# Attention with a tanh cap and a spectral mix: sums of exponentials in halves in two early slots, and a later tanh in one slot of each batch

## The chip, the cores and the metric

The kernel runs on one core of one Trainium2 chip. The metric is the device time of one execution in microseconds (us). A time quoted for a kernel is the median of several runs, and a profile is one execution of its own. A difference of about 0.2% (1.9 us here) is what a measurement of this kernel can tell from none.

## The reference

There are 8 batches of 12 heads, 448 positions and a head size of 64, all in float32. The core of the computation is:

```python
scores = cap * np.tanh(scale * (q @ k.T) / cap)
attn = np.exp(scores - scores.max(-1)); attn /= attn.sum(-1) + 1e-9
x = attn @ v                       # heads side by side: 448 x 768 per batch
theta = x @ w_theta
y = w_tok_r @ (x * cos(theta)) + w_tok_i @ (x * sin(theta))
u = x + y
out = u + np.maximum(u @ w_ch, 0)
```

For a cap of at most 64 the kernel leaves the subtraction of the maximum out (the cap is 30 here). The products of the second half use each float32 operand as a rounded part and a remainder, so one product takes three matmuls.

## The kernel before

**Slots.** The program is one written order of work, cut into slots. Slot s computes the scores of head pair s, in two halves of two key chunks each. The name s2_1 means the second half of pair 2. Slot s also multiplies the exponentials of pair k = s - 1 with the values (`av`, tile `a`) and adds up their sums (`sums`, tile `r`) by matmuls with a matrix of ones. There are 48 head pairs, six to a batch. Slots 0 to 7 are the opening (`start`): no batch is complete yet, and the vector engine splits the weights for the later products into rounded part and remainder (tags th, ch and tk in the table `WEIGHTS`). From slot 8 on, six slots make up one batch of the second half, with `part` 0 to 5. Part 2 (slots 10, 16, 22, ... 46) holds the second group of transposes and the first mixing products.

**Order.** The schedule is manual: each engine (PE for matmuls, ACT for activations, DVE for vector work, SP for issuing transfers) runs its instructions in the order in which the code records them, and waits where an operand or a buffer isn't ready. So an instruction that is recorded late holds nothing ahead of it, and one that waits holds everything behind it on its engine.

**Buffers.** The score tile `s` has one buffer of four PSUM banks. The matmuls of the next half can start only when the tanh (L219) has read the half before. The other PSUM tiles (`a`, `r`, `th`, `t`, `mx`, `ch`) share four single banks in turn. The tiles `p` of exponentials have two tags of three buffers: `p`, and `xhl`, which is also used for the split x. The function `apart` says which pairs of the first batch take `xhl`. The tiles `bc` have two buffers.

**The sums of the first batch.** For the first six pairs, two pairs share one tile `r`. In slots 2, 4 and 6 (k odd) the sums of both pairs are made: a group of 16 matmuls from the first halves ahead of the second scores, and a group from the second halves behind them. The reciprocal `ri` (L296, `invert`) follows in the same slot on DVE, four transfers spread it over the partitions (`bc`, L300), and `norm` (L304) multiplies x by it. After that `split_x` (L313 on ACT, L314 on DVE) makes the rounded x and its remainder: pairs 0 to 3 at the end of slot 6, pairs 4 and 5 at the end of slot 7.

**Part 2.** After the second scores come seven transposes of z (`t`, L355), the rounding of their result by ACT (`zh`, L356), the remainder by DVE (`zl`, L357), the reciprocal, and the mixing products (`mx`, L364 to L366), 21 matmuls each. On ACT the tanh of the second scores stands ahead of the rounding.

Of the kernel before, what the change touches and what calls it, by code (L numbers as in the profile page):

```python
# [16 lines left out]
AF = mybir.ActivationFunctionType  # L17
# [15 lines left out]
WHOLE = 14  # L33
# [3 lines left out]
def softcap_attn_then_spectral_mix(ctx, tc, qk2, v, cap, w_theta, w_tok, w_ch, ident, outT):  # L37
    nc = tc.nc
    B, NP, P, _, S = qk2.shape
    D = P // 2  # L40
    CP = v.shape[2]
# [4 lines left out]
    NS = B * NP  # L46
# [14 lines left out]
    qscale = const.tile([P, 1], F32, name="qscale")  # L61
# [20 lines left out]
    def fill(n):  # L82

        t = psM.tile([P, 512], F32, tag="m", name=f"fill{len(fills)}")
        fills.append(t)
        for _ in range(n):
            nc.tensor.matmul(t[:32, :CP], ones_sb, ones_sb[:, :1].broadcast_to([CP, CP]), start=True, stop=True)
# [8 lines left out]
    class Split:  # L96
# [20 lines left out]
        def split(self):  # L117
            t, hi, lo, hw, lw = self.t, self.hi, self.lo, self.hw, self.lw
            ti = t.bitcast(I32)
            nc.vector.tensor_scalar(ti, hw.bitcast(I32), 3, None, op0=ALU.logical_shift_left)  # L120
            nc.vector.scalar_tensor_tensor(ti, hw.bitcast(I32), -(2**31), ti, op0=ALU.bitwise_and, op1=ALU.bitwise_or)
            nc.vector.tensor_scalar(hw.bitcast(I32), ti, -(2**23), None, op0=ALU.bitwise_and)
            nc.vector.scalar_tensor_tensor(lw, lw.bitcast(U32), 2.0**-52, hw, op0=ALU.mult, op1=ALU.mult)
            if self.act:
                nc.scalar.copy(hi, t)
            else:
                nc.vector.tensor_copy(hi, t)
            nc.vector.tensor_tensor(t, t, hi.bitcast(F32), op=ALU.subtract)
            nc.vector.tensor_tensor(lo, t, lw, op=ALU.add)
# [35 lines left out]
    def weights(s, pos):  # L165
        for word in WEIGHTS.get((s, pos), "").split():
            step = steps[word[-3:-1], int(word[-1])]
            {">": step.load, "*": step.scale, "#": step.vscale}.get(word[0], step.split)()
# [4 lines left out]
    state = {}  # L173
# [3 lines left out]
    def load_qk(k):  # L177

        if 0 < k < WHOLE:
            raw[k] = wk.tile([P, 2, S], F32, tag=("hi", "lo")[k % 2], name=f"qk{k}", bufs=1)  # L180
        else:
            raw[k] = qk_sb
        nc.sync.dma_start(raw[k], qk2[k // NP, k % NP])

    def load_v(k):
        vt[k] = wk.tile([CP, 2, NCH, D], F32, tag="v", name=f"v{k}", bufs=2)
        nc.sync.dma_start(vt[k], v[k // NP, k % NP])
# [7 lines left out]
        if k + 1 < NS:  # L195
            load_qk(k + 1)

    def apart(k):


        return k < NP and k % 2 == 0

    def qk_half(k, half):

        sp = psS.tile([P, 2, 2, 512], F32, tag="s", name=f"s{k}_{half}")
        if apart(k):
            pp = wk.tile([CP, 2, 2, S], F32, tag="xhl", name=f"p{k}_{half}", bufs=3)
        else:
            pp = wk.tile([CP, 2, 2, S], F32, tag="p", name=f"p{k}_{half}", bufs=3)
        pt[k, half] = pp  # L210
        for i in range(2):
            ks = slice((2 * half + i) * CP, (2 * half + i + 1) * CP)
            products = ((raw, raw),) if k < WHOLE else ((hi, hi), (lo, hi), (hi, lo))
            for n, (kk, qq) in enumerate(products):
                for hh in range(2):
                    rows = slice(hh * D, (hh + 1) * D)
                    nc.tensor.matmul(sp[:CP, i, hh, :S], kk[k][rows, 1, ks], qq[k][rows, 0, :],  # L217
                                     start=n == 0, stop=n == len(products) - 1)
        nc.scalar.activation(pp, sp[:CP, :, :, :S], AF.Tanh, scale=qscale[:CP])  # L219

    def exp_half(k, half):

# [40 lines left out]
    def sum_pairs(ks, r, halves=(0, 1)):  # L263

        if ks[0] in pst:
            addends = [([pst.pop(k) for k in ks], True, True)]
        else:
            addends = [([pt[k, c // 2][:, c % 2] for k in ks], c == 0, c == NCH - 1) for c in range(NCH) if c // 2 in halves]
        for tiles, start, stop in addends:
            for k, a in zip(ks, tiles):  # L270
                for hh in range(2):
                    i = 2 * (k % 2) + hh
                    nc.tensor.matmul(r[32 * i : 32 * i + 32, :S], ones_sb, a[:, hh, :], start=start, stop=stop)  # L273

    def sums(k, halves=(0, 1)):

        alone = state["general"] or NP <= k < DIRECT
        if not alone and k % 2 == 0:
            return
        if state["general"] and 0 not in halves:  # L280
            return
        if (k % 2 == 0 or not alone) and 0 in halves:
            state["r"] = psM.tile([P, 512], F32, tag="m", name=f"r{k}")
        sum_pairs((k,) if alone else (k - 1, k), state["r"], halves)

    def invert(k):

        if k % 2 == 0:
            return
        r = state.pop("r")  # L290
        ri = wk.tile([P, S], F32, tag="ri", name=f"ri{k}", bufs=1)
        if state["general"]:
            nc.vector.tensor_scalar_add(ri, r[:, :S], 1e-9)
            nc.vector.reciprocal(ri, ri)
        else:
            nc.vector.reciprocal(ri, r[:, :S])  # L296
        for n in (k - 1, k):
            bc[n] = wk.tile([P, S], F32, tag="bc", name=f"bc{n}", bufs=2)
            for i in range(2):
                nc.sync.dma_start(bc[n][i::2, :], ri[D * (n % 2) : D * (n % 2) + D, :])  # L300
# [92 lines left out]
    def us(b, j):  # L393
        split_x(b, j, "us")

    def pipeline(general):
        state["general"] = general
        load_v(0)
        load_qk(1)
        for step in (("tk", 0), ("tk", 1)):  # L400
            steps[step].load()

        for s in range(FIRST + 6 * B):
            k = s - 1
            b, part = divmod(s - FIRST, 6)
            live = s < NS
            start = s < FIRST
            if s == 0:
                fill(FILL["first scores"])
            if live:  # L410
                qk_half(s, 0)
            if s == 0:
                fill(FILL["half"])
            if start:
                weights(s, "a")
                exp_half(s, 0)
            if 0 <= k < NS:
                av(k)
            if not start:
                weights(s, "a")  # L420
            if not start and part == 4:
                for j in range(NJ // 2, NJ):
                    us(b, j)
            if s + 1 < NS:
                load_v(s + 1)
            if 0 <= k < NS:
                sums(k, (0,) if start else (0, 1))
                if not start and part != 2:
                    invert(k)
            if live:  # L430
                qk_half(s, 1)
            if s == 0:
                fill(FILL["slot"])
            if 0 <= k and start:
                sums(k, (1,))
            if s + 2 <= WHOLE:
                load_qk(s + 2)
            if WHOLE <= s + 1 < NS and (start or part != 2):
                prep(s + 1)
            weights(s, "b")  # L440
            if 0 <= k and start:
                invert(k)
            script = ["B", "a", "b"] if start else part_scripts(b)[part]
            for i, e in enumerate(script):
                if not start and i == len(script) - 1:
                    weights(s, "c")
                    if s % 2 == 1 and s <= NS + 1:
                        norm(s - 3)
                        norm(s - 2)
                if isinstance(e, str):  # L450
                    if live:
                        if e in "AB":
                            exp_half(s, "AB".index(e))
                        else:
                            add_half(s, "ab".index(e))
                else:
                    e[0](b, e[1])
                if part == 2 and i == 0 and not start:
                    if 0 <= k < NS:
                        invert(k)  # L460
                    if WHOLE <= s + 1 < NS:
                        prep(s + 1)
            if start:
                weights(s, "c")
                for n in {4: (0, 1), 5: (2, 3), 7: (4, 5)}.get(s, ()):
                    norm(n)
                for j in {6: range(4), 7: range(4, NJ)}.get(s, ()):
                    split_x(0, j, "xs")
# [53 lines left out]
```

## Time and profile before

| what | value |
|---|---|
| median of 3 runs | 964.53 us (964.43 to 966.29) |
| the profiled execution's own time | 966.27 us |
| its span, first to last instruction | 964.5 us |
| PE busy | 945.6 us (98%) |
| DVE busy | 640.8 us (66%) |
| ACT busy | 590.5 us (61%) |
| granted TensorE clock | 0.997 |
| transfers | 68.68 MB, mean 71 GB/s |

The busy share of PE is near its limit over the whole span, so what remains to be looked at are the few places where PE sits idle. A row of the timeline has the start, the length, the engine, the line, the operation and its tiles, and in brackets how long the engine sat idle before it and what ended that. The ends of matmuls are modelled, so lengths of PE rows overlap, and distances between the starts of rows are the safer measure.

### The profile page before, as it was taken

The numbers are of one execution on the slowest core, as the hardware profiler recorded it, in microseconds if no ns is written. First come the engines' busy times: TensorE is split into PE (matmuls) and PEld (weight loads), VectorE is DVE, ScalarE is ACT, GpSimd is POOL, SyncE is SP. The second block draws the span as 40 slices with busy tenths as digits, with TensorE's granted clock in tenths as the row PEclk, the third lists the DMA queues.
The fourth block names the chain that finished last, engine by engine and source line by source line (L and its number), as shares of the span: only waits on it lengthen the run. The fifth ranks groups of instructions, "written<-read, shape, count | busy, mean of one in ns | idle before, by whom it ended". The sixth has DMA issues, their size and how long they took to land.

```text
span 964.5 us, 12776 instructions
## 1 busy us (share of the span) xinstructions
PE 945.6 (98%) x5224; PEld 697.3 (72%) x5224; DVE 640.8 (66%) x877; ACT 590.5 (61%) x609; POOL 0.4 (0%) x6
## 2 busy tenths in 40 slices
PE   8999999999999999999999999999999999999997
PEld 4234766677778777777787687767777877789897
DVE  5998787885855757756766559656585576664541
ACT  6888784667654687546963578456775558722520
POOL 0000000000000000000000000000000000000000
PEclk9999999999999999999999999999999999999999
DMA  7564122330113212132122221033011321001001
GB/s 252 193 194 138 34 82 94 112 103 30 49 39 105 67 39 63 32 98 67 32 66 68 77 67 48 29 87 94 31 49 39 105 68 39 20 15 62 0 1 61
DMA packets 30739, 68.68 MB, mean 71 GB/s; under 512 B 4304, under 2 KB 16720, under 8 KB 30672
## 3 DMA queue, kind: packets, MB, share of 16 engines
q1 hardware_dynamic: 30672, 67.78, 23.0%
q8 instruction: 43, 0.70, 0.3%
q14 instruction: 24, 0.20, 0.1%
HBM read 45.74 MB, written 11.01 MB: 59 GB/s over the span
## 4 chain that ended last, share of the span: by engine, by line
PE 88%; DVE 6%; ACT 4%; issue 1%; POOL 0%; POOLq 0%
PE a L257 15%; PE s L217 14%; PE mx L364 6%; PE mx L366 6%; PE mx L365 6%; PE th L322 6%; PE ch L322 6%; PE ch L324 6%; PE th L323 6%; PE ch L323 6%; PE th L324 6%; PE t L355 3%; PE r L273 3%; ACT p L219 2%; DVE ri L296 2%
## 5 line engine op out<-in xcount | busy, mean ns | idle before, releaser
L219 ACT ACTIVATE p<-s,qscale 112x1792 f32<-112x1792 f32 x96 | 168.7, 1757 | 168.7 <-PE s L217 168.7
L225 ACT ACTIVATE p<-p,cap_sb 112x1792 f32<-112x1792 f32 x96 | 170.6, 1790 | 0.6
L257 PE MATMUL a<-p,v 112*64 112x448 f32 x768 | 154.9, 545 | 0.0
L364 PE MATMUL mx<-wtk_h,zh 128*128 128x448 f32 x336 | 126.8, 377 | 5.4 <-DVE ri L296 3.6
L366 PE MATMUL mx<-wtk_h,zl 128*128 128x448 f32 x336 | 123.6, 368 | 0.0
L365 PE MATMUL mx<-wtk_l,zh 128*128 128x448 f32 x336 | 123.5, 367 | 0.0
L257 PEld LDWEIGHTS a<-p,v 112*64 112x64 f32 x768 | 50.9, 136 | 86.9 <-issue 77.1
L322 PE MATMUL th<-xs,wth_h 128*128 128x448 f32 x288 | 106.9, 371 | 0.0
L322 PE MATMUL ch<-us,wch_h 128*128 128x448 f32 x288 | 106.8, 371 | 0.0
L324 PE MATMUL ch<-us,wch_l 128*128 128x448 f32 x288 | 105.5, 366 | 0.0
L323 PE MATMUL th<-xs,wth_h 128*128 128x448 f32 x288 | 105.4, 366 | 0.0
L323 PE MATMUL ch<-us,wch_h 128*128 128x448 f32 x288 | 105.3, 366 | 0.0
L324 PE MATMUL th<-xs,wth_l 128*128 128x448 f32 x288 | 105.3, 366 | 0.0
L250 DVE TENSOR_TENSOR ps<-ps,p 112x896 f32<-112x896 f32 x80 | 87.0, 1087 | 1.4
L296 DVE RECIPROCAL ri<-r 128x448 f32<-128x448 f32 x24 | 70.8, 2952 | 12.0 <-PE r L273 11.9
L335 DVE SCALAR_TENSOR_TENSOR g_sb<-g_sb 128x448 f32<-128x448 f32 x48 | 29.9, 624 | 65.8 <-ACT g_sb L334 65.4
L364 PEld LDWEIGHTS mx<-wtk_h,zh 128*128 128x128 f32 x336 | 63.6, 189 | 11.9 <-issue 5.0
L357 DVE TENSOR_TENSOR zl<-t,zh 128x512 fp32r<-128x512 f32 x96 | 55.2, 616 | 24.5 <-ACT zh L356 24.5
L375 DVE SCALAR_TENSOR_TENSOR x<-ch,x 128x448 f32<-128x448 f32 x48 | 29.8, 620 | 59.0 <-PE ch L324 59.0
L366 PEld LDWEIGHTS mx<-wtk_h,zl 128*128 128x128 f32 x336 | 63.5, 189 | 5.4
L365 PEld LDWEIGHTS mx<-wtk_l,zh 128*128 128x128 f32 x336 | 63.7, 190 | 4.9
L322 PEld LDWEIGHTS ch<-us,wch_h 128*128 128x128 f32 x288 | 54.1, 188 | 9.6 <-issue 4.6
(75 smaller groups left out, 1377.8 us busy)
## 6 DMA issues: line engine op xcount, KB each, us to landing
qk_sb<-in_qk SPq DMA_DIRECT2D x35, 448.0 KB, 3.4
v<-in_v SPq DMA_DIRECT2D x48, 224.0 KB, 2.5
bc<-ri SPq DMA_DIRECT2D x96, 112.0 KB, 2.3
out_dram<-x SPq DMA_DIRECT2D x48, 224.0 KB, 1.9
qk<-in_qk SPq DMA_DIRECT2D x13, 448.0 KB, 3.4
g_sb<-in_wth SPq DMA_DIRECT2D x6, 768.0 KB, 5.4
g_sb<-in_wch SPq DMA_DIRECT2D x6, 768.0 KB, 4.7
swk_raw<-in_wtok SPq DMA_DIRECT2D x7, 448.0 KB, 4.1
```

Of the source, the lines that this page charges most:

```text
L217: nc.tensor.matmul(sp[:CP, i, hh, :S], kk[k][rows, 1, ks], qq[k][rows, 0, :], start=n == 0, stop=n == len(products) - 1)
L219: nc.scalar.activation(pp, sp[:CP, :, :, :S], AF.Tanh, scale=qscale[:CP])
L225: nc.scalar.activation(pp, pp, AF.Exp, scale=cap_sb[:CP])
L250: nc.vector.tensor_tensor(pst[k], pst[k], pt[k, 1][:, i], op=ALU.add)
L257: nc.tensor.matmul(acc[hh * D : (hh + 1) * D, :S], va[:, hh, c, :], pt[k, c // 2][:, c % 2, hh, :], start=c == 0, stop=c == NCH - 1)
L296: nc.vector.reciprocal(ri, r[:, :S])
L322: nc.tensor.matmul(acc[:, :S], wh[:, j, ms], t[:, 0, :], start=j == 0, stop=False)
L323: nc.tensor.matmul(acc[:, :S], wh[:, j, ms], t[:, 1, :], start=False, stop=False)
L324: nc.tensor.matmul(acc[:, :S], wl[:, j, ms], t[:, 0, :], start=False, stop=j == NJ - 1)
L364: nc.tensor.matmul(acc[:, :S], zh[:, c, :], wtk_h[:, c, :], start=c == 0, stop=False)
L365: nc.tensor.matmul(acc[:, :S], zh[:, c, :], wtk_l[:, c, :], start=False, stop=False)
L366: nc.tensor.matmul(acc[:, :S], zl[:, c, :], wtk_h[:, c, :], start=False, stop=c == NC2 - 1)
```

## The change

It has two parts.

**Sums in halves.** For pairs 0 and 1, and for pairs 2 and 3 (`split`: k = 1 and k = 3), the group from the first halves now stands behind the second scores of slots 2 and 4, and the group from the second halves behind the second scores of the slots after, 3 and 5. The reciprocal moves one slot later with them. The products `norm` of pairs 2 and 3 move from slot 5 to slot 6. The tiles of exponentials live longer for it, and `apart` gives other halves the tag `xhl`.

**Tanh later.** In part 2 the tanh of the second scores is recorded after the first group of transposes, behind the rounding of their result. This holds in the seven slots 10, 16, ... 46, which have scores of their own.

```diff
-    def apart(k):
-        return k < NP and k % 2 == 0
+    def apart(k, half):
+        return (k, half) in ((0, 0), (0, 1), (2, 0), (3, 0), (4, 0), (5, 0), (5, 1))
...
-        nc.scalar.activation(pp, sp[:CP, :, :, :S], AF.Tanh, scale=qscale[:CP])
+        return lambda: nc.scalar.activation(pp, sp[:CP, :, :, :S], AF.Tanh, scale=qscale[:CP])
...
+    def split(k):
+        return k in (1, 3) and not state["general"]
...
-                sums(k, (0,) if start else (0, 1))
+                if not start or not split(k):
+                    sums(k, (0,) if start else (0, 1))
                 if not start and part != 2:
                     invert(k)
+            late = not start and part == 2
             if live:
-                qk_half(s, 1)
+                tanh = qk_half(s, 1)
+                if not late:
+                    tanh()
...
             if 0 <= k and start:
-                sums(k, (1,))
+                if split(k):
+                    sums(k, (0,))
+                elif split(k - 1):
+                    sums(k - 1, (1,))
+                else:
+                    sums(k, (1,))
...
-            if 0 <= k and start:
-                invert(k)
+            if 0 <= k and start and not split(k):
+                invert(k - 1 if split(k - 1) else k)
...
-                if part == 2 and i == 0 and not start:
+                if late and i == 0:
+                    if live:
+                        tanh()
                     if 0 <= k < NS:
                         invert(k)
...
-                for n in {4: (0, 1), 5: (2, 3), 7: (4, 5)}.get(s, ()):
+                for n in {4: (0, 1), 6: (2, 3), 7: (4, 5)}.get(s, ()):
                     norm(n)
```

On PE, slots 2 and 3 before (each row of `r` stands twice, once for each head of a pair; the repeats are left out):

```order
L273 MATMUL r1_254<-p0_0_133,ones_sb_83 32x448 x2
L273 MATMUL r1_254<-p1_0_184,ones_sb_83 32x448 x2
...
L217 MATMUL s2_1_263<-qk2_170 112x448 x4
L273 MATMUL r1_254<-p0_1_153,ones_sb_83 32x448 x2
L273 MATMUL r1_254<-p1_1_205,ones_sb_83 32x448 x2
...
L217 MATMUL s3_0_298<-qk3_211 112x448 x4
L257 MATMUL a2_307<-p2_0_233,v2_202 64x448 x4
L257 MATMUL a2_307<-p2_1_264,v2_202 64x448 x4
L217 MATMUL s3_1_320<-qk3_211 112x448 x4
L217 MATMUL s4_0_349<-qk4_278 112x448 x4
```

and now:

```order
L217 MATMUL s2_1_254<-qk2_170 112x448 x4
L273 MATMUL r1_261<-p0_0_133,ones_sb_83 32x448 x2
L273 MATMUL r1_261<-p1_0_184,ones_sb_83 32x448 x2
...
L217 MATMUL s3_0_282<-qk3_211 112x448 x4
L257 MATMUL a2_291<-p2_0_233,v2_202 64x448 x4
L257 MATMUL a2_291<-p2_1_255,v2_202 64x448 x4
L217 MATMUL s3_1_304<-qk3_211 112x448 x4
L273 MATMUL r1_261<-p0_1_153,ones_sb_83 32x448 x2
L273 MATMUL r1_261<-p1_1_205,ones_sb_83 32x448 x2
...
L217 MATMUL s4_0_349<-qk4_270 112x448 x4
```

Slot 2 has one group of sums in place of two, and slot 3 one in place of none. Slots 4 and 5 read the same way.

On DVE, around the end of slot 6 before, from the last step of a weight split (L129) to the remainders of x:

```order
L129 TENSOR_TENSOR wth_l_78<-g_sb1_87 128x6x128
L296 RECIPROCAL ri5_526<-r5_492 128x448
L314 TENSOR_TENSOR xs0_0_536<-x0_200,xs0_0_536 128x448
L314 TENSOR_TENSOR xs0_0_536<-x1_250,xs0_0_536 128x448
L314 TENSOR_TENSOR xs0_2_541<-x2_316,xs0_2_541 128x448
```

and now, where the lines of the changed kernel are L300 for the reciprocal, L308 for `norm` and L318 for the remainders:

```order
L129 TENSOR_TENSOR wth_l_78<-g_sb1_87 128x6x128
L300 RECIPROCAL ri5_524<-r5_490 128x448
L308 TENSOR_TENSOR x2_300<-bc2_461,x2_300 128x448
L308 TENSOR_TENSOR x3_367<-bc3_464,x3_367 128x448
L318 TENSOR_TENSOR xs0_0_536<-x0_200,xs0_0_536 128x448
L318 TENSOR_TENSOR xs0_0_536<-x1_250,xs0_0_536 128x448
```

The products of pairs 2 and 3 now stand behind the third reciprocal, and ACT's rounding of x2 and x3 (not shown, its order is unchanged) needs them. The second reciprocal, ri3, now stands where these products stood, ahead of the last split of w_theta.

On ACT, slot 16 (part 2) before:

```order
L260 COPY x15_1780<-a15_1771 128x448
L219 ACTIVATE p16_1_1790<-s16_1_1789,qscale_70 112x1792
L356 CAST zh1_1_1804<-t1_1_0_1806 128x512
L356 CAST zh1_1_1804<-t1_1_4_1813 128x384
L341 ACT_TABLE_LOAD
```

and now:

```order
L260 COPY x15_1780<-a15_1771 128x448
L360 CAST zh1_1_1803<-t1_1_0_1805 128x512
L360 CAST zh1_1_1803<-t1_1_4_1812 128x384
L219 ACTIVATE p16_1_1790<-s16_1_1789,qscale_70 112x1792
L345 ACT_TABLE_LOAD
```

One instruction has moved past two, and nothing else on ACT has moved in the whole program. PE and DVE keep their order in these slots.

More of the change, by code (lines that the diff above doesn't have):

```diff
@@ L196, in prep @@
             load_qk(k + 1)
-    def apart(k):
-        return k < NP and k % 2 == 0
+    def apart(k, half):
+        return (k, half) in ((0, 0), (0, 1), (2, 0), (3, 0), (4, 0), (5, 0), (5, 1))
     def qk_half(k, half):
         sp = psS.tile([P, 2, 2, 512], F32, tag="s", name=f"s{k}_{half}")
-        if apart(k):
+        if apart(k, half):
             pp = wk.tile([CP, 2, 2, S], F32, tag="xhl", name=f"p{k}_{half}", bufs=3)
@@ L410, in pipeline @@
             if live:
-                qk_half(s, 0)
+                qk_half(s, 0)()
             if s == 0:
@@ L434, in pipeline @@
             if 0 <= k and start:
-                sums(k, (1,))
+                if split(k):
[4 more added lines that the diff above has]
+                    sums(k, (1,))
             if s + 2 <= WHOLE:
                 load_qk(s + 2)
-            if WHOLE <= s + 1 < NS and (start or part != 2):
+            if WHOLE <= s + 1 < NS and (not late):
                 prep(s + 1)
             weights(s, "b")
-            if 0 <= k and start:
-                invert(k)
+            if 0 <= k and start and not split(k):
+                invert(k - 1 if split(k - 1) else k)
             script = ["B", "a", "b"] if start else part_scripts(b)[part]
```

## The prediction

> **What bounds the kernel now.** I read the page first, then the list of waits of PE, then the timeline at the places that the list names.
>
> ```profile
> PE 945.6 (98%) x5224; PEld 697.3 (72%) x5224; DVE 640.8 (66%) x877; ACT 590.5 (61%) x609; POOL 0.4 (0%) x6
> PE s L217 <- ACT p L219: 6.7, 7, 1.9
> PE mx L364 <- DVE ri L296: 3.6, 7, 0.5
> ```
>
> PE is busy for 98% of the span, so only its idle time can be won. The two wait rows (total us, times, longest) hold most of that idle time. Both belong to places that the change touches: the next scores waiting for a tanh, and a mixing product waiting for a reciprocal.
>
> **Sums in halves, the PE side.** These are the rows of slots 2 to 5 on PE and ACT.
>
> ```profile
> 27.95 1.71 PE L273 MATMUL r<-p,ones_sb 112*32 112x448 f32 x16
> 29.59 1.76 PE L217 MATMUL s<-qk 64*112 64x448 f32 x8
> 31.28 1.71 PE L273 MATMUL r<-p,ones_sb 112*32 112x448 f32 x16
> 31.40 1.75 ACT L219 ACTIVATE p<-s,qscale 112x1792 f32<-112x1792 f32 x1 [2.49 <-PE s L217]
> 33.21 1.76 PE L217 MATMUL s<-qk 64*112 64x448 f32 x8 [0.21 <-ACT p L219]
> ...
> 39.87 1.75 ACT L219 ACTIVATE p<-s,qscale 112x1792 f32<-112x1792 f32 x1 [0.50 <-PE s L217]
> 41.67 1.76 PE L217 MATMUL s<-qk 64*112 64x448 f32 x8 [1.86 <-ACT p L219]
> ...
> 49.97 1.75 ACT L219 ACTIVATE p<-s,qscale 112x1792 f32<-112x1792 f32 x1 [1.47 <-PE s L217]
> 51.78 1.76 PE L217 MATMUL s<-qk 64*112 64x448 f32 x8 [0.21 <-ACT p L219]
> ```
>
> In slot 2 the group of sums at 27.95 pushes the second scores to 29.59, 1.64 us later. The tanh at 31.40 waits for these scores with ACT idle for 2.49 us, and the first scores of slot 3 wait for that tanh. Without the group, s2_1 starts at 27.95. The buffer is free then: by 28.91 (31.40 - 2.49) ACT had finished the tanh of the first half and also what stands behind it. The moved group now stands where the other one stood, at 31.28, and is hidden behind the tanh as that one was. So tanh and next scores come 1.64 us earlier: 33.21 becomes 31.57.
>
> Slot 3 keeps its length, 41.67 - 33.21 = 8.46 us. It ends with a wait of 1.86 us for the tanh at 39.87. The group that now arrives there takes 1.64 us from its start to the next start (27.95 to 29.59), and so it fits into the 1.86 with 0.2 left, as the bracket 0.21 at 33.21 and 51.78 already shows for slots that have such a group. If that cover were gone, it would cost 1.64.
>
> Slot 4 is like slot 2, but ACT sat idle for only 1.47 us before its tanh, so ACT sets the gain: 1.47. Slot 5 is like slot 3. Together PE and ACT arrive 1.64 + 1.47 = 3.1 us earlier at slot 6, if nothing else holds them.
>
> **Sums in halves, the DVE side.** What else may hold them is DVE, which works off the weight splits nearly without a pause. These are the corner rows of its work until slot 7, with the ACT and PE rows that hang on it.
>
> ```profile
> 31.24 0.96 DVE L129 TENSOR_TENSOR wth_l<-g_sb 128x768 fp32r<-128x768 f32 x1
> 34.88 0.61 ACT L112 ACTIVATE swk_raw<-swk_raw 128x448 f32<-128x448 f32 x1
> 36.36 0.38 DVE L120 TENSOR_SCALAR swk_t<-swk_raw 128x448 int32<-128x448 int32 x1
> 46.43 0.56 DVE L120 TENSOR_SCALAR g_sb<-g_sb 128x768 int32<-128x768 int32 x1 [0.82 <-ACT g_sb L112]
> 51.98 2.95 DVE L296 RECIPROCAL ri<-r 128x448 f32<-128x448 f32 x1
> 54.84 1.08 DVE L304 TENSOR_TENSOR x<-bc,x 128x448 f32<-128x448 f32 x2
> 55.85 0.38 DVE L120 TENSOR_SCALAR swk_t<-swk_raw 128x448 int32<-128x448 int32 x1
> 63.23 1.15 DVE L304 TENSOR_TENSOR x<-bc,x 128x448 f32<-128x448 f32 x2
> 64.30 0.56 DVE L120 TENSOR_SCALAR g_sb<-g_sb 128x768 int32<-128x768 int32 x1
> 70.23 2.96 DVE L296 RECIPROCAL ri<-r 128x448 f32<-128x448 f32 x1 [0.32 <-PE r L273]
> 72.52 1.95 ACT L313 CAST xs<-x 128x448 fp32r<-128x448 f32 x4
> 74.37 1.75 ACT L219 ACTIVATE p<-s,qscale 112x1792 f32<-112x1792 f32 x1
> 80.73 1.76 PE L217 MATMUL s<-qk 64*112 64x448 f32 x8 [0.52 <-ACT p L219]
> ```
>
> Pairs 2 and 3 are now multiplied by their reciprocals behind the third reciprocal, and ACT rounds x2 and x3 ahead of the tanh of slot 7. When does DVE get there? Its first reciprocal has moved back, so after 32.20 (31.24 + 0.96) it goes on with the next splits. The first of them needs ACT's scaled weight (34.88 + 0.61 = 35.49 before, now 1.64 earlier), so it starts at 33.85. From there DVE has no reason to pause. The first moved reciprocal needs sums that end before the first scores of slot 4 (41.67 - 1.64 = 40.0), and by the steps below DVE arrives there at 43.1. The second needs sums that end before the first scores of slot 6 (51.78 - 3.1 + 8.46 = 57.1), and DVE arrives at 59.9.
>
> The steps, each from row to row: two splits 9.25 (36.36 to 46.43, less the idle 0.82), reciprocal 2.86 (51.98 to 54.84), split 5.55 (46.43 to 51.98), norm of pairs 0 and 1 1.01 (54.84 to 55.85), two splits 7.38 (55.85 to 63.23), reciprocal 2.86, split 5.61 (64.30 to 70.23, less 0.32), reciprocal 2.86. The sum is 37.4, so the norm of pair 2 starts at 71.2 and ends at 71.8 (half of 1.15).
>
> Before, ACT began the four roundings at 72.52. Without DVE it could now begin them at 69.4 (3.1 earlier). It does the first two, waits, and begins the third at 71.8. A rounding takes 0.46 ((74.37 - 72.52) / 4), so the tanh of slot 7 starts at 72.8 in place of 74.37: **1.6 us** of the 3.1 remain. PE follows ACT in this slot (the wait of 0.52 at 80.73), so what ACT wins PE wins. Upper bound: 3.1, if DVE isn't what holds ACT. Lower bound: 0, if DVE is 1.6 us slower over these 37.4 us than the rows make it. I take 1.6, since every step of it has a row.
>
> Two things are costed at nothing. The transfers of `bc` for pairs 4 and 5 now wait on SP for the norm of pair 3, which frees their buffers at 72.3, about a microsecond after the third reciprocal has ended. The loads queued behind them wait as long. What they feed, the norm at the end of slot 7, comes only after the row at 80.73. The new places of the `p` tiles: each buffer is written again only after the sums that read it, at least one half slot later.
>
> **Tanh later.** These are the rows of slot 16, then two of slot 10.
>
> ```profile
> 245.06 0.98 PE L355 MATMUL t<-ident_sb,g_sb 128*128 128x128 f32 x7
> 245.17 1.76 ACT L219 ACTIVATE p<-s,qscale 112x1792 f32<-112x1792 f32 x1 [1.76 <-PE s L217]
> 245.30 1.08 DVE L346 TENSOR_TENSOR g_sb<-g_sb,x 128x896 f32<-128x896 f32 x1
> 246.83 0.95 ACT L356 CAST zh<-t 128x512 fp32r<-128x512 f32 x2
> 247.44 1.16 DVE L357 TENSOR_TENSOR zl<-t,zh 128x512 fp32r<-128x512 f32 x2 [1.05 <-ACT zh L356]
> 248.51 2.95 DVE L296 RECIPROCAL ri<-r 128x448 f32<-128x448 f32 x1
> 250.16 0.93 PE L355 MATMUL t<-ident_sb,g_sb 128*128 128x128 f32 x7
> 250.42 1.31 ACT L342 ACTIVATE g_sb<-g_sb 128x1344 f32<-128x1344 f32 x1
> 251.60 0.44 PE L364 MATMUL mx<-wtk_h,zh 128*128 128x448 f32 x1 [0.51 <-DVE ri L296]
> 253.51 1.08 DVE L346 TENSOR_TENSOR g_sb<-g_sb,x 128x896 f32<-128x896 f32 x1
> 255.95 0.93 PE L355 MATMUL t<-ident_sb,g_sb 128*128 128x128 f32 x7
> 256.59 0.97 ACT L356 CAST zh<-t 128x512 fp32r<-128x512 f32 x2 [0.91 <-PE t L355]
> 256.63 0.45 PE L364 MATMUL mx<-wtk_h,zh 128*128 128x448 f32 x1
> ...
> 130.82 1.16 DVE L357 TENSOR_TENSOR zl<-t,zh 128x512 fp32r<-128x512 f32 x2 [0.48 <-ACT zh L356]
> 134.99 0.44 PE L364 MATMUL mx<-wtk_h,zh 128*128 128x448 f32 x1 [0.52 <-DVE ri L296]
> ```
>
> The chain is tanh, rounding, remainder, reciprocal, mixing product: the product at 251.60 takes the bank of `r`, which the reciprocal frees. Its start follows that of the reciprocal by 251.60 - 248.51 = 3.09. With the tanh out of the way, the rounding starts 0.64 after the transposes, as at 256.59 (255.95 + 0.64): at 245.70. The remainder follows 0.61 behind (246.83 to 247.44), at 246.31, and there DVE is just done with the row at 245.30. The reciprocal follows 1.07 behind that (247.44 to 248.51), at 247.38, and the product may start at 250.47.
>
> PE itself is ready when its transposes allow: where nothing waits, the product starts 0.68 after them (255.95 to 256.63), which gives 250.16 + 0.68 = 250.84. This is the later of the two, so PE sets the pace again, with 0.37 to spare, and the product comes 251.60 - 250.84 = 0.76 earlier. In slot 10 DVE had only 0.48 of idle to give, so I take 0.5. The other five slots have the same 0.51 wait in the same chain (7 waits of 3.6 in all). The sum is 6 x 0.76 + 0.5 = **5.1 us**.
>
> By the idle column alone the gain would be 3.6, and the sum of both parts 5.2 in place of 6.7. The Trainium skill, page "Perfetto Trace Analysis", section "Tensor Engine Instruction (MATMUL, LD_WEIGHTS)", says that the end of a matmul in a profile is an estimate; an idle time counted from such an end is short of the stall by as much as the modelled end is late. The trace agrees in that 256.63 lies inside the row that begins at 255.95 and lasts 0.93.
>
> What the tanh delays: it runs from about 246.6 to 248.3 now (0.95 of rounding from 245.70), against 246.93 as its end before and 247.78 as the end of the rounding. The sine behind it slips by about 0.5, so that it ends at 252.2 in place of 251.73 (250.42 + 1.31). Who waits for it is the DVE row at 253.51, which had other work ahead; that work is now earlier by about 1.1, so the row starts at about 252.4. The slip stays hidden, with 0.2 left. The next scores need the tanh's buffer only more than 10 us later. Lower bound of this part: 3.0, if each stall shrinks by 0.43 and no more. Upper bound: 5.3, seven times 0.76.
>
> **The sum.** 1.6 + 5.1 = 6.7 us. The span of 964.5 becomes 957.8, and the profiled execution's own 966.27 about 959.6. The median of the runs, 964.53, lies 1.7 below the profiled execution, so the same gain is taken from it: **957.8 us**.
>
> **Rivals.**
>
> (a) DVE doesn't hold the opening, and all 3.1 us arrive: 964.53 - 8.2 = 956.3. For it: every number on the PE side is a plain row. Against it: DVE pauses for only 0.82 and 0.32 between 36.36 and 72.3 in the rows above, and the moved norm stands at the very end of that work.
>
> (b) The opening gives nothing, because DVE runs 1.6 us or more later than summed: 964.53 - 5.1 = 959.4. For it: eight steps in a row, each with a semaphore. Against it: the steps are measured from start to start, with these in them.
>
> (c) In part 2 another wait takes the place of the reciprocal, for instance the rounding's own PSUM bank or the remainder on DVE. Then the seven stalls stay, only the opening gains, and the time is 964.53 - 1.6 = 962.9, within 0.2% (1.93 us). For it: the spare is only 0.37 in slot 16 and nothing in slot 10. Against it: each link has a measured distance in the same slot.
>
> (d) Slower: the rounding of x2 holds ACT far longer than summed, because the norm of pair 2 is late. ACT, and with it PE, then loses a microsecond for each microsecond. The place is the end of slot 6. The gain of the opening is gone when the norm ends after 73.4, and the kernel is slower than before once it ends after 78.5 (73.4 + 5.1). With 81.0 the time would be 964.53 + 2.5 = 967.0. For it: the transfers of `bc` for pairs 2 and 3 now stand on SP behind two weight loads which wait for their own buffers. Against it: those buffers are free once DVE has done the two splits ahead of the second reciprocal itself, so they can't hold it.
>
> **How the numbers follow.** My forecast, a gain of about 5 to 7.5 us, has 0.66. Rival (a) has 0.10, (b) 0.10, (c) 0.10, (d) 0.04. The predicted time is 957.8. The range runs from (a), 956.3, to 961.5, where the opening gives nothing and part 2 its lower bound of 3.0. It leaves out (c) and (d), 0.14 together. Faster by over 0.2%: 0.66 + 0.10 + 0.10 = 0.86. Within 0.2%: 0.10. Slower: 0.04.
>
> **What would show it.** Part by part: the waits of PE for the tanh in slots 3 and 5 fall from 1.86 to about 0.2, and the scores at 41.67 and 51.78 start near 40.0 and 48.7. ACT waits for about 1.4 us between the second and third rounding of x near 70 to 72, released by the norm, and the tanh at 74.37 starts near 72.8. The row of PE's waits for the reciprocal disappears or keeps one entry near 0.2 (slot 10). The distance from the second transposes to the second mixing product in slot 16 falls from 1.44 to about 0.7. The prediction is wrong if the waits for the reciprocal are replaced by others at L364 in the same slots, or if DVE is idle for more than a microsecond between 34 and 72.

## The result and the profile after

The changed kernel takes 959.36 us (median of 5 runs, 956.1 to 959.81), the kernel before beside it 966.14 us (5 runs, 964.43 to 966.36). The ratio is 0.9925, with a 95% interval of 0.9909 to 0.9941, so the change gains 0.6% to 0.9%. The prediction's ratio was 957.8 / 964.53 = 0.9930. The profiled execution took 959.81 us with a span of 958.0; predicted were 959.6 and 957.8.

Single executions of one kernel differ by up to 3.7 us, which is more than some of the differences below. So each profiled execution is cut into four stretches at three rows of PE: the first scores of slot 2, the second scores of slot 8, and the first mixing product of the last batch. What happens before the first cut and after the third is the same work in both kernels.

| us | before the first scores of slot 2 | opening: to the second scores of slot 8 | batches: to the last batch's first mixing product | tail: to the end | span |
|---|---|---|---|---|---|
| before | 23.10 | 65.61 | 818.12 | 57.67 | 964.5 |
| after | 23.49 | 63.86 | 812.97 | 57.68 | 958.0 |
| difference | +0.39 | -1.75 | -5.15 | +0.01 | -6.5 |
| predicted | 0 | -1.6 | -5.1 | 0 | -6.7 |

The waits of PE after, with the same columns as before (total us, times, longest):

```profile
PE s L217 <- ACT p L219: 4.9, 8, 1.9
PE mx L368 <- DVE zl L361: 1.8, 1, 1.8
```

The row for the reciprocal, which had 7 waits of 3.6 us, is gone. The other one, a product of the last batch that waits for a remainder, stands as before. The waits for the tanh have become more in number and less in sum.

The opening on PE in the timeline after; to set a time beside one of before, take off 0.39.

```profile
23.49 1.76 PE L217 MATMUL s<-qk 64*112 64x448 f32 x8 [1.85 <-ACT p L219]
...
28.34 1.76 PE L217 MATMUL s<-qk 64*112 64x448 f32 x8
30.03 1.71 PE L273 MATMUL r<-p,ones_sb 112*32 112x448 f32 x16
30.14 1.76 ACT L219 ACTIVATE p<-s,qscale 112x1792 f32<-112x1792 f32 x1 [0.85 <-PE s L217]
31.95 1.76 PE L217 MATMUL s<-qk 64*112 64x448 f32 x8 [0.22 <-ACT p L219]
...
38.49 1.71 PE L273 MATMUL r<-p,ones_sb 112*32 112x448 f32 x16
40.42 1.76 PE L217 MATMUL s<-qk 64*112 64x448 f32 x8 [0.22 <-ACT p L219]
...
48.95 1.76 PE L217 MATMUL s<-qk 64*112 64x448 f32 x8 [0.28 <-ACT p L219]
```

In slot 2 the second scores (28.34) have no group of sums ahead of them now; one stands behind them at 30.03, under the tanh, and the other in slot 3 at 38.49, where the wait of 1.86 has shrunk to 0.22. The scores at 40.42 and 48.95 answer to 41.67 and 51.78 before: less 0.39, they come 1.64 and 3.22 us earlier.

The corner of DVE's work at which the prediction's sum of eight steps began, and then the end of slot 6 and slot 7 after, on DVE, ACT and PE:

```profile
34.26 0.39 DVE L120 TENSOR_SCALAR swk_t<-swk_raw 128x448 int32<-128x448 int32 x1 [1.20 <-ACT swk_raw L112]
...
68.56 2.95 DVE L300 RECIPROCAL ri<-r 128x448 f32<-128x448 f32 x1
69.71 1.01 ACT L317 CAST xs<-x 128x448 fp32r<-128x448 f32 x2
71.43 1.09 DVE L308 TENSOR_TENSOR x<-bc,x 128x448 f32<-128x448 f32 x2
72.02 1.09 ACT L317 CAST xs<-x 128x448 fp32r<-128x448 f32 x2 [1.30 <-DVE x L308]
73.02 1.75 ACT L219 ACTIVATE p<-s,qscale 112x1792 f32<-112x1792 f32 x1
...
79.37 1.76 PE L217 MATMUL s<-qk 64*112 64x448 f32 x8 [1.16 <-ACT p L219]
79.85 0.83 ACT L125 CAST wch_h<-g_sb 128x768 fp32r<-128x768 f32 x1 [0.53 <-DVE g_sb L121]
```

ACT rounds x0 and x1 at 69.71, waits 1.30 us for the norm of pair 2, and rounds the other two at 72.02. Here 1.5 of the 3.2 us that PE and ACT had won are lost: the scores at 79.37 are 1.75 us earlier than at 80.73 before.

Slot 16, and then slot 10, after:

```profile
243.83 0.97 ACT L360 CAST zh<-t 128x512 fp32r<-128x512 f32 x2 [2.35 <-PE t L359]
244.45 1.15 DVE L361 TENSOR_TENSOR zl<-t,zh 128x512 fp32r<-128x512 f32 x2
244.68 1.77 ACT L219 ACTIVATE p<-s,qscale 112x1792 f32<-112x1792 f32 x1
245.52 2.95 DVE L300 RECIPROCAL ri<-r 128x448 f32<-128x448 f32 x1
248.24 0.93 PE L359 MATMUL t<-ident_sb,g_sb 128*128 128x128 f32 x7
248.92 0.45 PE L368 MATMUL mx<-wtk_h,zh 128*128 128x448 f32 x1
...
129.98 2.95 DVE L300 RECIPROCAL ri<-r 128x448 f32<-128x448 f32 x1
132.19 0.93 PE L359 MATMUL t<-ident_sb,g_sb 128*128 128x128 f32 x7
133.07 0.44 PE L368 MATMUL mx<-wtk_h,zh 128*128 128x448 f32 x1
134.39 1.09 DVE L350 TENSOR_TENSOR g_sb<-g_sb,x 128x896 f32<-128x896 f32 x1 [0.99 <-ACT g_sb L346]
```

In slot 16 the product follows its transposes by 0.68 (1.44 before), and the reciprocal by 3.40, so it is ready 0.31 before PE is. In slot 10 the product follows the reciprocal by exactly 3.09, so DVE still sets the time there; 0.88 lies between transposes and product, 1.45 before. The 0.20 that is left of that stall doesn't show in the idle column.

### The profile page after: what moved, and what is told of

Read it like the earlier page. It is cut to its first block, busy times and chain, and to the rows that moved or that the text cites. A ratio compares the mean times of both kernels' runs of the same rounds, so it can differ in the third digit from the quotient of the medians.

```text
span 958.0 us, 12766 instructions
## 1 busy us (share of the span) xinstructions
PE 944.5 (99%) x5224; PEld 698.0 (73%) x5224; DVE 641.3 (67%) x877; ACT 590.0 (62%) x609; POOL 0.4 (0%) x6
## 4 chain that ended last, share of the span: by engine, by line
PE 90%; DVE 6%; ACT 3%; issue 1%; DMA 0%; SPq 0%; POOL 0%; DVEq 0%; POOLq 0%
PE a L257 14%; PE s L217 13%; PE mx L368 7%; PE mx L370 7%; PE mx L369 7%; PE th L326 6%; PE ch L326 6%; PE ch L328 6%; PE th L327 6%; PE th L328 6%; PE ch L327 6%; PE t L359 4%; PE r L273 2%; DVE ri L300 1%; ACT p L219 1%; PE fill L87 1%
## 5 line engine op out<-in xcount | busy, mean ns | idle before, releaser
L300 DVE RECIPROCAL ri<-r 128x448 f32<-128x448 f32 x24 | 70.8, 2951 | 10.1 <-PE r L273 9.9
L360 ACT CAST zh<-t 128x512 fp32r<-128x512 f32 x96 | 45.8, 532 | 32.6 <-PE t L359 32.6
```

## Experiments

These are the stretches of the eight kernels that were run, cut at the same rows, and their times. The ratio is to the kernel before on the same chip, whose medians were 964.52 us of 17 runs (beside the first four kernels) and 966.53 us of 11 runs (beside the last four).

| kernel | before slot 2 | opening | batches | tail | median us | ratio, 95% interval |
|---|---|---|---|---|---|---|
| first part alone | 23.35 | 63.92 | 818.09 | 56.24 | 963.04 | 0.9975 [0.9965, 0.9986] |
| second part alone | 23.05 | 65.62 | 812.96 | 56.17 | 960.05 | 0.9947 [0.9932, 0.9962] |
| norm ahead | 22.80 | 63.76 | 813.06 | 56.18 | 958.38 | 0.9931 [0.9915, 0.9946] |
| norm ahead, split later | 22.78 | 62.42 | 812.93 | 56.17 | 956.70 | 0.9911 [0.9894, 0.9928] |
| reciprocal early | 22.56 | 65.61 | 812.85 | 57.78 | 959.67 | 0.9935 [0.9922, 0.9948] |
| cover gone | 22.61 | 66.00 | 813.00 | 57.79 | 959.67 | 0.9931 [0.9915, 0.9947] |
| last transposes early | 23.35 | 62.41 | 811.00 | 56.24 | 954.44 | 0.9879 [0.9865, 0.9893] |
| last stall filled | 21.24 | 62.41 | 812.93 | 56.22 | 956.11 | 0.9898 [0.9884, 0.9912] |

The stretch before slot 2 and the tail move by up to 2.3 and 1.6 us between kernels whose work there is the same; they come back in the last section. The opening and the batches repeat within 0.2 us wherever the edit leaves them alone.

### Each part alone

The first kernel has the sums in halves, with the tanh of part 2 back in its place:

```diff
                 tanh = qk_half(s, 1)
-                if not late:
-                    tanh()
+                tanh()
...
                 if late and i == 0:
-                    if live:
-                        tanh()
```

> The change's first part alone: the sums in halves, with the tanh of part 2 where it was before. Theory (the two parts add up; DVE holds the opening at the end of slot 6): a gain of 1.6 us against the kernel before (span about 962.9), with the seven waits of the mixing products for the reciprocal back at 0.51 each and, in the profile, a wait of ACT of about 1.3 us between the second and third rounding of x. Rival (the opening gives nothing, and part 2 gives all): span 964.5 plus or minus 0.3.

The second has the later tanh, with the sums, the norms and the places of the `p` tiles (`apart`) of the kernel before:

```diff
-        return (k, half) in ((0, 0), (0, 1), (2, 0), (3, 0), (4, 0), (5, 0), (5, 1))
+        return k < NP and k % 2 == 0
...
     def split(k):
-        return k in (1, 3) and not state["general"]
+        return False
...
-                for n in {4: (0, 1), 6: (2, 3), 7: (4, 5)}.get(s, ()):
+                for n in {4: (0, 1), 5: (2, 3), 7: (4, 5)}.get(s, ()):
```

> The change's second part alone: the tanh of part 2 behind the rounding, with the sums of the first batch as before. Theory (counted from start to start, six times 0.76 and once 0.5): a gain of 5.1 us, span about 959.4. Rival (counted by the idle column): 3.6 us, span about 960.9. In both, PE has no wait for the reciprocal left at the mixing products; the distance from the second transposes to the second mixing product in slot 16 falls from 1.44 to 0.68.

With the first part alone the opening is 1.69 us shorter and the batches are as before (818.09). Its list of waits and its slot 16 show the reciprocal again:

```profile
PE mx L368 <- DVE ri L300: 3.6, 7, 0.5
250.14 0.44 PE L368 MATMUL mx<-wtk_h,zh 128*128 128x448 f32 x1 [0.51 <-DVE ri L300]
```

With the second part alone the opening is as before (65.62) and the batches are 5.16 us shorter. The parts add up: -1.69 and -5.16 against -1.75 and -5.15 together. This also decides between the two counts for the second part. The waits that vanish read 3.6 us in the idle column, and the program becomes 5.16 us shorter, which is what the distances from start to start had given (5.1).

### Is it the reciprocal?

The second part moves a tanh on ACT, but the theory is that PE waits for a PSUM bank which DVE's reciprocal frees late. Then it must help as much to leave the tanh alone and put the reciprocal ahead of the remainder on DVE. This is the kernel before with that one move:

```diff
                 sums(k, (0,) if start else (0, 1))
-                if not start and part != 2:
+                if not start:
                     invert(k)
...
                 if part == 2 and i == 0 and not start:
-                    if 0 <= k < NS:
-                        invert(k)
```

> The kernel before (tanh and sums where they were), with one move: in part 2 the reciprocal is recorded ahead of the transposes' remainder on DVE, not behind it. Theory (the second mixing product waits for the bank of r, which the reciprocal frees, and the tanh matters only because the reciprocal stands behind it): the reciprocal of slot 16 starts near 246.4 in place of 248.51, the remainder follows near 249.3 to 250.4, and the product may start at 250.84: the seven waits of 0.51 are gone without the tanh having moved, the gain is about 5 us, span about 959.5. Rival (the product waits for the remainder or for something else behind the tanh, and the reciprocal is only the last that the profile names): the waits stay, or come back under the name of the remainder, and the span stays within 1 us of 964.5.

All seven waits are gone and the batches are 5.27 us shorter (812.85), with ACT's order as before. Slot 16 of this kernel:

```profile
243.95 1.76 ACT L219 ACTIVATE p<-s,qscale 112x1792 f32<-112x1792 f32 x1 [1.76 <-PE s L217]
245.09 2.95 DVE L296 RECIPROCAL ri<-r 128x448 f32<-128x448 f32 x1
245.60 0.96 ACT L356 CAST zh<-t 128x512 fp32r<-128x512 f32 x2
```

The reciprocal starts ahead of the rounding, and the tanh runs first, as it did before. So what the product waited for is the end of the reciprocal, and the tanh mattered only because rounding and remainder, and behind them the reciprocal, stood after it. That it is the bank of `r` that the product needs is argued from the code: the product uses no result of the reciprocal. The edit may also change which bank the product takes, and this run doesn't separate the two.

### What held the opening at 1.75 of 3.2

In the prediction it is the norm of pair 2, which stands on DVE behind the third reciprocal. This kernel does the norms of pairs 2 and 3 ahead of that reciprocal:

```diff
             weights(s, "b")
+            if s == 6:
+                norm(2)
+                norm(3)
             if 0 <= k and start and not split(k):
                 invert(k - 1 if split(k - 1) else k)
...
-                for n in {4: (0, 1), 6: (2, 3), 7: (4, 5)}.get(s, ()):
+                for n in {4: (0, 1), 7: (4, 5)}.get(s, ()):
```

> The changed kernel with one move: the norm of pairs 2 and 3 stands ahead of the third reciprocal on DVE in slot 6, not behind it. Theory (the norm behind the reciprocal is what holds ACT at the end of slot 6): ACT's wait of 1.3 us between the roundings of x is gone, the tanh of slot 7 starts near 71.6 in place of 73.02, and the first scores of slot 8 near 78.0 in place of 79.37. But DVE reaches the split of ch0 no earlier, ACT's cast in the middle of it waits for that (79.85 as in the changed kernel), the exp behind the cast ends near 82.4 as now, and the products of slot 7 need that exp: so the second scores of slot 8 start only about 0.2 earlier than 87.35, and the span is about 957.8. Rival (the rounding's wait was the only hold): the whole 1.4 arrives, span about 956.6. Other rival (DVE doesn't matter here): no change in the start of slot 7.

Slot 7 and the beginning of slot 8 in it, on ACT and PE (its first scores of slot 2 start at 22.80, so 0.69 is to be added to a time to set it beside the changed kernel):

```profile
69.02 1.95 ACT L317 CAST xs<-x 128x448 fp32r<-128x448 f32 x4
70.87 1.75 ACT L219 ACTIVATE p<-s,qscale 112x1792 f32<-112x1792 f32 x1
77.24 1.76 PE L217 MATMUL s<-qk 64*112 64x448 f32 x8 [0.55 <-ACT p L219]
79.19 0.83 ACT L125 CAST wch_h<-g_sb 128x768 fp32r<-128x768 f32 x1 [2.00 <-DVE g_sb L121]
79.93 1.79 ACT L225 ACTIVATE p<-p,cap_sb 112x1792 f32<-112x1792 f32 x1
81.77 1.72 PE L257 MATMUL a<-p,v 112*64 112x448 f32 x8 [1.11 <-ACT p L225]
```

The four roundings run without a pause, and tanh and first scores come 1.44 us earlier than in the changed kernel (77.24 + 0.69 against 79.37). But ACT then stands 2.00 us at its step of the split of w_ch0, a cast that waits for DVE, and PE waits 1.11 for the exp behind it. In the end the opening is 0.10 us shorter. The second hold is there in the changed kernel too: the 0.53 at 79.85.

The next kernel also moves that split (`ch0` in the table of the weights' work) from slot 7 to the beginning of slot 8:

```diff
-        ... (7, "b"): "tk4 >tk6 ch0", (7, "c"): "*tk5",
+        ... (7, "b"): "tk4 >tk6", (8, "a"): "ch0", (7, "c"): "*tk5",
```

> As the kernel with the norm ahead of the third reciprocal, and in addition the split of ch0 moves from slot 7 to the beginning of slot 8, so that ACT's cast no longer stands ahead of the exp of slot 7 and DVE reaches the norm of pairs 4 and 5 about 4.9 us earlier. Theory (two holds by DVE, one behind the other, cost what the opening didn't give): first scores of slot 8 near 78.0, second scores near 86.0 in place of 87.35, span about 956.6, which is 1.4 below the changed kernel and 7.9 below the kernel before. Rival (a third hold follows at once, DVE's split in slot 8 delaying the reciprocal of pairs 6 and 7 and the work of theta): the 1.4 is given back by slot 9, where PE's wait of 0.27 ahead of the first transposes grows to more than 1, and the span stays at about 958.

```profile
77.20 1.79 ACT L225 ACTIVATE p<-p,cap_sb 112x1792 f32<-112x1792 f32 x1
78.91 3.23 PE L257 MATMUL a<-p,v 112*64 112x448 f32 x16
82.64 0.84 ACT L125 CAST wch_h<-g_sb 128x768 fp32r<-128x768 f32 x1
```

Now the exp at 77.20 comes ahead of the cast at 82.64 and PE doesn't wait at 78.91. The opening is 62.42, 3.19 us shorter than before: all that PE and ACT had won by slot 6 (3.22). The batches stay at 812.93, so nothing of it is given back later.

### Is the wait in slots 3 and 5 the cover?

The group of sums that was moved into slots 3 and 5 is costed at nothing, because it runs while PE would wait for a tanh. Here the same group stands ahead of that slot's second scores:

```diff
+            if 0 <= k and start and split(k - 1):
+                sums(k - 1, (1,))
             late = not start and part == 2
...
                 if split(k):
                     sums(k, (0,))
-                elif split(k - 1):
-                    sums(k - 1, (1,))
-                else:
+                elif not split(k - 1):
                     sums(k, (1,))
```

> The changed kernel, with the second group of sums of pairs 0 and 1 and of pairs 2 and 3 ahead of the second scores of slots 3 and 5, not behind them. Theory (the groups are free only behind the tanh's wait): each of slots 3 and 5 grows by 1.64, the first scores of slot 4 start 1.6 later than 40.42, those of slot 6 3.2 later than 57.42, ACT no longer waits at the roundings of x because it arrives late itself, and the opening gains nothing: 1.4 to 1.6 slower than the changed kernel, about 5 faster than the kernel before (span about 959.5). Rival (the order of the groups doesn't matter as long as there is one to a slot): same as the changed kernel.

Slot 3 of this kernel:

```profile
35.93 1.71 PE L273 MATMUL r<-p,ones_sb 112*32 112x448 f32 x16
37.57 1.76 PE L217 MATMUL s<-qk 64*112 64x448 f32 x8
39.38 1.76 ACT L219 ACTIVATE p<-s,qscale 112x1792 f32<-112x1792 f32 x1 [2.15 <-PE s L217]
41.19 1.76 PE L217 MATMUL s<-qk 64*112 64x448 f32 x8 [1.86 <-ACT p L219]
```

The wait of 1.86 is back, and slots 3 and 5 are 1.64 and 1.63 us longer than in the changed kernel: the price that the prediction named. The opening is 66.00, not merely what it was before but 0.39 worse. Most of that arises at the roundings of x, where the expectation had ACT no longer waiting. DVE now waits 1.47 us for the sums of slot 6 and starts its third reciprocal at 69.80; the norm of pair 2 still stands behind it, and ACT still waits for the norm:

```profile
73.27 1.09 ACT L317 CAST xs<-x 128x448 fp32r<-128x448 f32 x2 [0.15 <-DVE x L308]
```

The tanh of slot 7 starts 2.17 us after the first rounding, in place of 1.85 before. The medians (959.67 here, 959.36 with the cover) don't show the loss of 2.14 against the changed kernel, since single executions of this kernel lie between 957.95 and 961.31; the stretches do.

### The last wait

One wait of PE over 1.5 us is left outside the opening, in the last batch: the first mixing product waits 1.83 us for a remainder, since all transposes of that part stand directly ahead of it. This kernel starts from "norm ahead, split later" and puts them earlier, for the last batch alone:

```diff
             [(sincos, 0), (theta, 3), (rotate, 0), "A", ... (theta, 5), (transp, 0), (rotate, 2)]
+            if b + 1 < B else
+            [(sincos, 0), (rotate, 0), (rotate, 1), (theta, 3), (theta, 4), (transp, 0), (theta, 5), (rotate, 2)],
```

> The kernel with both holds of the opening taken away (norm first, ch0 later), and one more move: in the last batch, which has no scores to cover a wait, the first transposes stand ahead of the last theta product, and the first two rotations ahead of the work on theta 3. Theory (the wait of 1.83 at the first mixing product is the chain transposes, rounding, remainder right ahead of it, and 3.7 us of theta work can cover it): the wait is gone, 1.8 less than the kernel with both holds away (span about 952.5 where the clock stays up). In executions with a granted clock of 0.997, the clock fell to half for about 3 us right behind that wait, at a cost of about 1.5 us; without the wait no execution should show it, so all runs should lie close together. Rival (the wait only moves, to the transposes for their rotation): span about 954.3, wait under another name.

```profile
891.53 0.93 PE L359 MATMUL t<-ident_sb,g_sb 128*128 128x128 f32 x7
894.54 1.15 DVE L361 TENSOR_TENSOR zl<-t,zh 128x512 fp32r<-128x512 f32 x2
895.96 0.93 PE L359 MATMUL t<-ident_sb,g_sb 128*128 128x128 f32 x7
896.76 0.47 PE L368 MATMUL mx<-wtk_h,zh 128*128 128x448 f32 x1
```

With the first transposes at 891.53 the remainder is under way while PE still works on the rotation angles, and the product at 896.76 follows its transposes without a wait. The batches lose 1.93 us. The four runs lie within 0.83 us, as expected; but those of the kernel that it starts from, which has the wait, lie within 0.74. This is the fastest kernel of the study, 954.44 us, 1.2% below the kernel before.

The other kernel starts from "norm ahead, split later" too, leaves the wait where it is and only keeps PE busy in it, with eight small products of ones whose result nobody reads. The question was whether the wait lowers the clock behind it:

```diff
+                if late and i == 0 and not live:
+                    t = psS.tile([P, 2, 2, 512], F32, tag="s", name="fill_last")
+                    for _ in range(8):
+                        nc.tensor.matmul(t[:32, 0, 0, :CP], ones_sb, ones_sb[:, :1].broadcast_to([CP, CP]), start=True, stop=True)
```

> The kernel with both holds of the opening taken away, and in the wait of 1.83 us at the first mixing product of the last batch eight small matmuls of ones into the unused score buffer, whose result nobody reads. Theory (the clock falls because PE sits idle there): the same span as without them where the clock stays up, 954.3 plus or minus 0.3, and no execution with the clock at half behind the wait; the runs lie within 1 us of each other. Rival (the fall has nothing to do with the idle time): some executions still show it, and the runs spread over 1.5 us or more as those of the kernel before do (964.4 to 966.4).

The batches stay at 812.93, as they must, and the tail is 56.22. The runs still spread by 1.7 us (954.55 to 956.23), more than the one microsecond expected; at least the beginning of the program varies still, as the last section shows. Nor does the run answer the question: in the kernel that it starts from, no run shows a low clock behind the wait either (last section), so there was nothing to take away.

## Why the prediction was right, point by point

- **Opening, PE and ACT: 1.64 + 1.47 = 3.1.** Measured 3.22 at the scores of slot 5. Slot 2 gave 1.64 as worked out. Slot 4 gave 1.58, 0.11 us more than the idle of ACT ahead of its tanh.
- **Opening, DVE: 1.6 of it remain.** Measured 1.75. The mechanism is the one named, ACT waits between the second and the third rounding (1.30; 1.4 was named), and with the norms ahead of the reciprocal that wait is gone. The sum over eight steps of DVE was 37.4 us; the norm at 71.43 comes 37.17 after the split at 34.26 where the sum began. The tanh of slot 7 starts at 73.02 - 0.39 = 72.63; 72.8 was predicted.
- **What the prediction missed there.** The prediction knows only one place where DVE holds ACT, the norm of pair 2. There are two. Without the norm's hold, the split of w_ch0 takes nearly all of it back (opening 63.76 in place of 63.86), and only when both were moved did the whole gain arrive. So the 1.6 hangs on the norm less than the prediction has it: with the norm early the opening still gives only 65.61 - 63.76 = 1.85, and the 3.1 of rival (a) was out of reach as long as the split stood where it did.
- **The cover in slots 3 and 5.** It is as described, 0.2 us of room and 1.64 us if it is gone.
- **Tanh later: 6 x 0.76 + 0.5 = 5.1.** Measured 5.15: slot 16 gave 0.76, slot 10 0.57, the other five 0.74 to 0.76, which is 5.07 in all; where the other 0.08 arise wasn't followed. The prediction's start-to-start count held; the idle column alone (3.6) would have been 1.5 us short. This agrees with what the prediction cites from the Trainium skill, that the end of a matmul in a profile is an estimate: waits that read 0.51 each were worth 0.76.
- **The slip of the sine stays hidden, with 0.2 left.** In slot 16 DVE doesn't wait for it, with 0.13 left (the sine ends at 250.40, DVE's row starts at 250.53). In slot 10 DVE's product at 134.39 waits 0.99 us for the sine, and PE waits for nothing there, so it costs nothing; but this room was counted in one slot and taken for all. The later transfers of `bc`, put at nothing, cost nothing: the norm of pairs 4 and 5 starts at 83.19 without a wait ahead of it.
- **The other rivals.** (b), a gain of nothing in the opening, is refuted by the 63.86. (c), the stalls under another name, by the list of waits and by the stretch of the batches. (d), a late norm, by the rounding at 72.02: the norm of pair 2 had ended by 72.02 - 0.39 = 71.63, where 73.4 would have used up the gain of the opening.
- **The base.** The sum was made against the profiled execution and carried over to a median that lay 1.7 us lower. Later runs of the kernel before lay between 962.9 and 966.9, most of them near 964.4 or near 966.4, so a distance of this size is chance: the same kernel beside the changed one had a median of 966.14. It is the ratio that can be compared.

## What to carry to other kernels

Count a stall from the start of the work that feeds it to the start of the work that waits, in a slot with the stall and in one without; the idle column was 30% short here. When work is taken off the engine that sets the pace, sum up the other engines' order from row to row to where they meet again, and look beyond the first meeting point: here the first hold, once removed, showed a second one six instructions behind the roundings on the same engine, which took back nearly all that the first had cost. Where executions scatter by as much as the effect, cut the profiled spans at the same rows and compare stretches.

## What the runs showed of the hardware

**A wait of 1.83 us can be followed by a low clock.** Of the eight profiled executions with the 1.83 us wait in the last batch, four (before, after, reciprocal early, cover gone) have a tail of 57.7 to 57.8 us and four a tail of 56.2. These are windows of the changed kernel behind that wait, which ends at 900.32. The columns are the window, its length, busy time with number of instructions for PE, its weight loads, DVE, ACT and POOL, then the granted clock, the share of DMA and GB/s.

```profile
901.00:902.00 1.00, 1.00 (x5) 0.92 (x5) 1.00 (x2) 1.00 (x2) 0.00 (x0) 0.74 0.00 0
902.00:903.00 1.00, 1.00 (x4) 0.88 (x4) 0.79 (x2) 0.40 (x1) 0.00 (x0) 0.50 0.00 0
903.00:904.00 1.00, 1.00 (x5) 0.88 (x3) 0.00 (x0) 0.00 (x0) 0.00 (x0) 0.50 0.00 0
904.00:905.00 1.00, 1.00 (x4) 0.92 (x3) 0.00 (x0) 0.00 (x0) 0.00 (x0) 0.55 0.00 0
905.00:906.00 1.00, 1.00 (x6) 0.93 (x6) 0.00 (x0) 0.00 (x0) 0.00 (x0) 1.00 0.00 0
```

About a microsecond after the wait has ended, the granted clock falls to 0.50, and it stays there for some 3.4 us: the four lower windows lose 0.26 + 0.50 + 0.50 + 0.45 = 1.71 us of clock, at half speed. The same stretch with the first part alone, where the same wait ends at 905.36:

```profile
904.00:908.00 4.00, 2.65 (x13) 2.46 (x14) 3.79 (x7) 3.44 (x5) 0.00 (x0) 1.00 0.00 0
908.00:912.00 4.00, 4.00 (x25) 3.69 (x24) 2.06 (x3) 0.97 (x2) 0.00 (x0) 1.00 0.00 0
```

Here the clock stays at 1.00. The Trainium skill, page "TensorE: Matmul & The Clock Gate", section "HAM oscillation — how this bites in real kernels", gives as the rule that PE mustn't be idle for more than about 3.4 us; the measurement differs in that the clock fell here although no wait of PE in this execution is longer than 1.9 us. That the low clock lasts about 3.4 us agrees with the length of window that the page gives. Waits of 1.85 us in the opening, as at 23.49, lowered no clock. That the wait is the cause isn't settled. The mean granted clock of an execution is 0.997 in the four profiles with the long tail and 0.999 or 1.000 in the others, and by this sign 39 of 71 executions with the wait had the fall, and none of eight without it. But both kernels without the wait start from "norm ahead, split later", which has the wait and shows 0.997 in none of its four executions. So the comparisons in which the wait alone goes show nothing of its effect; why the share differs between kernels stays open.

**The first microseconds differ from execution to execution.** The first scores after, and then those of "last stall filled":

```profile
5.43 3.33 PE L217 MATMUL s<-qk_sb 64*112 64x448 f32 x8
```

```profile
5.40 1.76 PE L217 MATMUL s<-qk_sb 64*112 64x448 f32 x8 [0.33 <-DMA qk_sb<-in_qk]
```

The same eight products take 3.33 us in one and 1.76 in the other, although the two kernels are the same up to there and the granted clock reads 1.00 in both; what decides it wasn't followed. The scores of slot 2 then start at 23.49 in the one and 21.24 in the other. Together with the tail that can make 3 to 4 us between two executions (2.25 + 1.5), over half of what the change gains.
